# Attention in front of two feed-forward layers: the first chunk divided by its softmax sums after the products with values, sums and their spread from TensorE, a new order

## The chip, the cores and the metric

The kernel runs on one core of a Trainium2 chip. The metric is the device time of one execution in microseconds. The engines are TensorE (PE; its weight loads are shown apart as PEld), VectorE (DVE), ScalarE (ACT), GpSimd (POOL) and SyncE (SP), which here issues the transfers (DMA).

## The reference

All numbers are fp32. Attention has 2 batches, 8 heads, 768 tokens and 64 dimensions a head. Each token sees the tokens nearer than 16 positions, and besides these 24 block keys (maxima over 32 keys), to whose scores log 32 is added, with block values (means over 32 values). The result, 1536 tokens by 512, goes through a gated layer of 1536 hidden units and a second layer of 2048.

```python
k_sum = k.reshape(B, H, nb, block, D).max(axis=3)
v_sum = v.reshape(B, H, nb, block, D).mean(axis=3)
scores_l = where(|i - j| < 16, scale * q @ k.T, -1e9)
scores_s = scale * q @ k_sum.T + log(block)
a = exp(scores_all - max); a = a / (sum(a) + 1e-09)
x = a @ concat([v, v_sum])            # -> (1536, 512)
x = (silu(x @ w_gate) * (x @ w_val)) @ w_out
h = x @ w_in                          # second layer
g = where(h >= 1, h, where(h <= -1, 0, (h + 1)**2 / 4))
out = g @ w_out2
```

## The kernel before

The 1536 tokens are cut into three chunks of 512. Chunk 0 goes through both layers in a plain form; chunks 1 and 2 are done together later in a form that needs fewer products. Attention works on pairs of heads (four) and segments of 256 tokens (two per chunk), so chunk 0 has eight segment jobs. In each, four windows of 64 queries meet 120 keys: 96 neighbours and 24 blocks (KN = 120).

A segment job is a row of stages, each a function in `stages`: `sc`, the scores on TensorE, two PSUM banks; `mx`, on VectorE, masks and scales a tile of 128 rows (two heads' windows) at a time, and takes the extremes, into `sm`; `ex`, the exponentials on ScalarE; `su`, the row sums on VectorE, in the first four segment jobs only (`wide`), while the others let ScalarE accumulate the sums; `iv`, the reciprocals; `no`, the multiplication of the weights with the reciprocals, on VectorE or GpSimd; `wt`, four transposes on TensorE; `pt`, the copy of the transposed weights to SBUF (`pT`). Then `av` multiplies them with the window's values, and for chunk 0 `xh` and `xl` split the result, channels by tokens, into a high and a low part, each in the reduced-precision format fp32r in which TensorE multiplies the layers (three products for one: high with high, high with low, low with high, `mm3`). `ve` puts the means of the block values beside the neighbours' values; `av` needs it. Weights of the layers are decoded from 64-bit words (`high`, `low`, `bits`) and split (`hi`, `lo`).

The order of all instructions is made by a planner (`Plan.emit`) when the program is built. It takes, again and again, the ready job with the least of planned start plus `urge` times rank, and puts it on the engine with the least of start plus a weighted cost. The ranks, and the jobs' times, are the constants of table `T` and the numbers in braces at each job. Rings (score tiles, PSUM banks, slots of SBUF) hold a job back until its place is free; chunk 0 may use eight banks, since the accumulators of the layers are not open then. Where the planner foresees that TensorE will wait, `bank` (line 296) puts in up to 14 transposes of the identity, the padding. Engines serve their queues in the planned order; semaphores make them wait where the plan was wrong.

Lines that the following speaks of: 296 padding; 577 `av`; 594 `xl`; 626 `sc`; 639 `mx`; 645 `su`; 651 `ex`; 657 and 659, 660 `iv`; 664 `no`; 672 `wt`; 385, 387 and 389 the helper `copy` on ScalarE, GpSimd and VectorE; 918 the helper `subtract`; 979 the products with the layers' weights; 483 the means of values; 514 the transposes of keys; 558 those of queries.

Of the kernel before, what the change touches and what calls it, by code (L numbers as in the profile page):

```python
# [25 lines left out]
 'urge': 0.00031,  # L26
 'weight': (0.672, 366.647, 0.107, 0.393),
# [3 lines left out]
 'd': (1603.21, 21201.717),  # L31
 'load': (2535.858, 1169.195),
 'high': (-317.411, 144.375),
 'bits': (-9479.17, 323.65),
 'keep': (-8824.092, -1262.662),
 'read': -21513.508,
 'hi': (-1775.607, 438.05),
 'lo': (1720.695, -1280.083),
 'head_rank': (-928.987, -10909.065, -11298.818, 1371.39),
 'half_rank': -8764.036,  # L40
 'start': 146.833,
 'unit': 2.295,
 'e0': 140.493,
 'a1': (66.347, 15.995),
 'a2': (120.489, 10.661),
 'x': (326.313, 950.529),
 'j': (573.745, 3379.756),
 'g': (0.575, 58.663),
 'q': (0.02, 0.075),
 'jr': (223.915, 25.793),  # L50
 'jw': (526.692, 905.968),
 'rw': 1427.588,
 'js': (-12378.664, 1097.852),
 'gh': (305.541, 615.993),
 'gl': -803.961,
 't': 255.967,
 'th': 1363.181,
 'tl': -46.182,
 'qp': (-25.993, -0.438, 3.895, 62.512, 43.492, -4.889, -18.174),
 'qf': 37.334,  # L60
 'qj': -997.531,
 'qa': 1676.758,
 'rs': 755.395,
 'rh': 472.89,
 'x2': 62.301,
 'r2': (-105.0, 2012.755),
 'first': (641.149, 531.258),
 'st_q': (2394.976, -370.146),
 'st_qt': (595.066, -1246.954),
 'st_sc': (-351.835, -992.682),  # L70
 'st_mx': (-696.018, -1785.299),
 'st_ex': (-1399.05, 2957.286),
 'st_iv': (-4718.413, -828.92),
 'st_no': (616.963, -14960.718),
 'st_wt': (-628.517, 19.831),
 'st_pt': (-29498.836, 337.373),
 'st_av': (213.136, -938.929),
 'st_xh': (-1380.886, -2003.135),
 'st_xl': (-1030.954, -12578.763),
 'kl': (-42201.382, -2356.932),  # L80
 'kp': (2529.629, -2690.699),
 'kt': (-5799.683, 2883.66),
 'km': (-12751.053, -745.621),
 'kc': (1095.192, -13449.83),
 'vl': (3292.292, -1209.876),
 'vm': (2875.792, 2369.738),
 'vs': -8200.552,
 'vo': (-8471.926, -9352.02),
 've': (-19.098, 1391.293),
 'ql': (-21759.128, -1085.432),  # L90
 'wl': (-2925.377, -25041.841),
 'wide': 4,
 'st_su': (810.604, 7542.977),
 'seg': (129.041, -64.326),
 'ko': (-3502.726, 21290.576)}
# [136 lines left out]
def tile_block_attention_ffn(  # L232
# [20 lines left out]
    nc = tc.nc  # L253
# [23 lines left out]
    ap_ = ctx.enter_context(tc.tile_pool(name="ap", bufs=2))  # L277
# [9 lines left out]
        "qT": 2, **T["rings"],  # L287
# [58 lines left out]
    for m, offs in enumerate(((0, WINDOW), (WINDOW, WINDOW), (WINDOW, 2 * WINDOW))):  # L346
# [9 lines left out]
        "big1", (1, (2 * WPS, H, D)), (2, (CH,)), (2, (2, S // P, D)), (2, (2 * D,)), (1, (2, NB + 32)), (1, (NB + 32,)))  # L356
    vall, qTs, kraws, vms, wavg, tavg = carved[0], carved[1:3], carved[3:5], carved[5:7], *carved[7:]
# [8 lines left out]
    n_steps, n_jobs = [0], [0]  # L366
# [178 lines left out]
    xt = {}  # L545
# [20 lines left out]
    def values(c, p, tag, one=None):  # L566

        px = bank(tag, "px")
        pend["px", c, p] = pend["px", c, p, one] = px
        for i, (b, s) in enumerate(chunk_segments(c)):  # L570
            if one not in (None, i):
                continue
            pT, vwin = pend.pop(("pT", b, s, p)), vwins[(b * NSEG + s) % 2]
            for w in range(WPS):
                col = i * SEG + w * QT
                for h in range(2):
                    nc.tensor.matmul(  # L577
                        px[h * D:(h + 1) * D, col:col + QT], vwin[0:KN, w, 2 * p + h],
                        pT[0:KN, 2 * h + w // 2, w % 2 * QT:(w % 2 + 1) * QT],
                        start=True, stop=True,  # L580
                    )
# [7 lines left out]
    def values_lo(c, p, i, *rings):  # L589
        x = xt[c][p]  # L590
        if rings:
            x.append(slot(rings[0], f"xl{p}", F32R))
        cols = slice(i * SEG, (i + 1) * SEG)
# [10 lines left out]
    def stages(b, s, p, wide, first=None):  # L604

        c, col = divmod(b * S + s * SEG, CH)
        v_ = shared[b, s, p] = {}

        def scores(*tags):
# [4 lines left out]
            v_["mx"] = ap_.tile([P, 2, WPS], F32, tag="mx", name="mx", bufs=4)  # L614
# [53 lines left out]
        def weights(tag, ring):  # L668
            v_["pT"] = pend["pT", b, s, p] = slot(ring, "pT").rearrange("p (w c) -> p w c", c=P)
            pt = v_["pt"] = bank(tag, "pt")  # L670
            for w in range(WPS):
                nc.tensor.transpose(pt[0:KN, w * P:(w + 1) * P], v_["sm"][:, w], ident)  # L672

        def weights_out(engine):
            pT = v_["pT"]
            copy(engine, pT[0:KN].rearrange("p w c -> p (w c)"), v_["pt"][0:KN, :])
# [3 lines left out]
            "ex": exps, "su": sums, "iv": inverse, "no": normalise,  # L680
            "wt": weights, "pt": weights_out,
# [7 lines left out]
        ("su", {"DVE": 0.65}, "st_su", ("ex",)),  # L689
# [3 lines left out]
        ("pt", {"ACT": 0.61, "DVE": 0.69}, "st_pt", ("wt",)),  # L693
    )
# [43 lines left out]
    def step_jobs(c, p, t, banks, after):  # L738
# [22 lines left out]
        if not c:  # L761
            for i, (b, s) in enumerate(segs):
                u = t + T["seg"][0] * i
                h = (*n, i)
                job(("av", *(h if not i else n)), {"PE": 0.56},
# [3 lines left out]
                av, xh, xl = (("av", *n), ("xh", *n), ("xl", *n)) if i else (  # L769
                    ("av", *h), ("xh", *h), ("xl", *h))  # L770
                job(xh, {"ACT": 0.4, "DVE": 0.42}, u + T["st_xh"][0],
                    lambda e, *rings, i=i: values_hi(c, p, i, e, *rings),
                    [av] + ([("xh", *n, 0)] if i else []), () if i else (XS,))
                job(xl, {"DVE": 0.42}, u + T["st_xl"][0],
                    lambda e, *rings, i=i: values_lo(c, p, i, *rings),
                    [xh] + ([("xl", *n, 0)] if i else []), () if i else (XS,), [(av, 0)])
# [22 lines left out]
    def segment_jobs(b, s, p, t, banks, done):  # L799
# [15 lines left out]
        wide = n_jobs[0] < T["wide"]  # L815
        n_jobs[0] += 1
        fns = stages(b, s, p, wide, one)
        for name, engines, dt, needs in STAGES:
            fn = fns[name]
            if name == "su" and not wide:  # L820
                continue
            if wide and name == "ex":
                engines = {"ACT": 0.95}
            if wide and name == "iv":
                engines, needs = {"DVE": 0.18}, ("su",)
            rank = plan.jobs["sc", *one][1] + 0.1 if one and name == "sc" else t + T[dt][c > 0]
            job((name, *n), engines, rank,
                (lambda e, *tags, fn=fn: fn(*tags)) if "PE" in engines else lambda e, *_, fn=fn: fn(e),
# [653 lines left out]
```

## Time and profile before

| | us |
|---|---|
| median of 3 runs | 613.23 (612.58 to 614.61) |
| the profiled execution | 613.35 |
| its span in the profile | 611.6 |

| engine | busy us | share of the span |
|---|---|---|
| PE | 599.6 | 98% |
| PEld | 494.2 | 81% |
| DVE | 493.2 | 81% |
| ACT | 359.1 | 59% |
| POOL | 35.9 | 6% |

The profile is one execution. Times in it count from the start of its span. A busy engine is one that has an instruction in work; matmuls overlap, and their ends are modelled, so a busy TensorE need not be one at its peak. The granted clock is TensorE's, 1.00 being 2.4 GHz and 0.50 being 1.2 GHz.

### The profile page before, as it was taken

Reading aid. Unit: us, or ns where it says so; the run is one execution under the profiler, and the core shown is the slowest. Engines: PE = TensorE matmul, PEld = TensorE weight load, DVE = VectorE, ACT = ScalarE, POOL = GpSimd, SP = SyncE. Lnnn points to the kernel's source line nnn. Section 1 sums busy time; section 2 is a strip of 40 time slices with the busy share of each in tenths; the row PEclk is TensorE's granted clock in tenths of the full one; section 3 lists DMA queues with packets and bytes.
Section 4 is the critical chain, followed back from the end, with each engine's and each line's share of the span. In section 5 each row is a group of like instructions: output and inputs, shape, how many; then the busy total and the mean of one; then the engine's idle time right before and its main releaser. Section 6 shows DMA issues by size and latency. Waiting matters only on the chain.

```text
span 611.6 us, 9465 instructions
## 1 busy us (share of the span) xinstructions
PE 599.6 (98%) x3554; PEld 494.2 (81%) x3554; DVE 493.2 (81%) x897; ACT 359.1 (59%) x650; POOL 35.9 (6%) x55
## 2 busy tenths in 40 slices
PE   7889999999999999999999999999999999999997
PEld 6588888888878888888888888888888888888886
DVE  5789888999898998998888878788888868857662
ACT  5886678878888874764444444332278565556112
POOL 4250001100000000000000001000000010001000
PEclk9799999999999999999999999999999999999999
DMA  9999999998999670441120221133310420021411
GB/s 217 285 267 249 340 318 358 370 338 284 253 315 308 234 275 1 173 145 62 69 70 0 70 105 69 35 103 104 137 36 0 128 80 35 0 70 45 163 35 69
DMA packets 82334, 94.99 MB, mean 155 GB/s; under 512 B 40432, under 2 KB 65264, under 8 KB 82288
## 3 DMA queue, kind: packets, MB, share of 16 engines
q1 hardware_dynamic: 82288, 94.39, 48.1%
q8 instruction: 28, 0.46, 0.3%
q14 instruction: 18, 0.15, 0.1%
HBM read 73.40 MB, written 20.97 MB: 154 GB/s over the span
## 4 chain that ended last, share of the span: by engine, by line
PE 93%; DVE 3%; ACT 1%; DMA 1%; SPq 1%; issue 0%; POOL 0%; ACTq 0%; DVEq 0%; POOLq 0%
PE acc_y L979 38%; PE qi L979 12%; PE qv L979 9%; PE qg L979 9%; PE pi L979 7%; PE pv L979 5%; PE pg L979 5%; PE px L577 2%; PE pt L672 1%; PE sc L626 1%; DMA big<-in_k_dram 1%; DVE wb L895 1%; DVE wA L389 1%; SPq L439 1%; PE pk L296 1%; ACT sm L651 1%
## 5 line engine op out<-in xcount | busy, mean ns | idle before, releaser
L979 PE MATMUL acc_y<-dd,h 128*128 128x512 f32 (+1 forms) x387 | 88.9, 387 | 0.0
L979 PEld LDWEIGHTS acc_y<-dd,h 128*128 128x128 f32 x387 | 72.4, 188 | 14.9
L979 PE MATMUL acc_y<-h,dd 128*128 128x512 f32 x288 | 66.5, 389 | 0.0
L385 ACT ACTIVATE dd<-wf 128x1024 fp32r<-128x1024 f32 x25 | 26.4, 1058 | 62.8 <-PE acc_y L979 62.8
L979 PEld LDWEIGHTS acc_y<-h,dd 128*128 128x128 f32 x288 | 54.1, 188 | 11.3
L979 PE MATMUL acc_y<-wA,h 128*128 128x512 f32 x192 | 46.3, 391 | 0.0
L979 PE MATMUL qi<-xj,wjs 128*128 128x512 f32 x192 | 45.8, 389 | 0.0
L979 PE MATMUL pi<-y,wA 128*128 128x512 f32 x128 | 42.8, 394 | 0.0
L979 PEld LDWEIGHTS qi<-xj,wjs 128*128 128x128 f32 x192 | 36.0, 188 | 7.5
L979 PEld LDWEIGHTS acc_y<-wA,h 128*128 128x128 f32 x192 | 35.8, 188 | 7.4
L895 DVE SCALAR_TENSOR_TENSOR wb<-dd 128x1024 int32<-128x1024 int32 x34 | 41.1, 1220 | 0.3
L918 DVE TENSOR_TENSOR wA<-wb,wA 128x1024 fp32r<-128x1024 f32 x31 | 37.6, 1223 | 1.9 <-ACT wA L385 1.4
L886 ACT ACTIVATE dd<-raw 128x1024 f32<-128x1024 f32 x34 | 38.3, 1139 | 0.2 <-DMA raw<-in_moe_w_val_dram 0.2
L979 PE MATMUL acc_y<-h,wA 128*128 128x512 f32 x144 | 36.8, 399 | 0.0
L979 PE MATMUL qg<-xj,wjs 128*128 128x512 f32 x144 | 36.5, 389 | 0.0
L979 PE MATMUL qv<-xj,wjs 128*128 128x512 f32 x144 | 36.4, 389 | 0.0
L979 PE MATMUL pg<-x,wA 128*128 128x512 f32 (+1 forms) x112 | 35.4, 371 | 0.5 <-DVE wA L918 0.5
L979 PE MATMUL qi<-xj,wjo 128*128 128x512 f32 x144 | 34.7, 389 | 0.0
L979 PE MATMUL pv<-x,wA 128*128 128x512 f32 (+1 forms) x112 | 34.2, 368 | 0.0
L918 DVE TENSOR_TENSOR dd<-wf,dd 128x1024 fp32r<-128x1024 f32 x27 | 33.0, 1224 | 0.4 <-ACT dd L385 0.3
L918 DVE TENSOR_TENSOR h<-r,h 128x512 fp32r<-128x512 f32 x45 | 30.9, 691 | 1.2
L979 PEld LDWEIGHTS qi<-xj,wjo 128*128 128x128 f32 x144 | 27.0, 188 | 5.6
(167 smaller groups left out, 1216.3 us busy)
## 6 DMA issues: line engine op xcount, KB each, us to landing
raw<-in_moe_w_out_dram SPq DMA_DIRECT2D x14, 1024.0 KB, 7.3
raw<-in_moe_w_in_dram SPq DMA_DIRECT2D x16, 512.0 KB, 6.6
wf<-kept_z SPq DMA_DIRECT2D x16, 512.0 KB, 3.2
raw<-in_moe_w_gate_dram SPq DMA_DIRECT2D x12, 512.0 KB, 8.1
raw<-in_moe_w_val_dram SPq DMA_DIRECT2D x12, 512.0 KB, 8.6
kept_g<-wb SPq DMA_DIRECT2D x12, 512.0 KB, 5.5
wj<-kept_g SPq DMA_DIRECT2D x12, 512.0 KB, 4.5
wf<-kept_o SPq DMA_DIRECT2D x12, 512.0 KB, 3.4
```

Of the source, the lines that this page charges most:

```text
L296: nc.tensor.transpose(t[:, 0:P], ident, ident)
L385: nc.scalar.activation(out, in_, AF.Copy, scale=scale)
L389: nc.vector.tensor_copy(out, in_)
L439: nc.sync.dma_start(out=vwin[0:KW, w], in_=bass.AP(src.tensor, src.offset, [[D, KW], [S * D, H], [1, D]]),)
L577: nc.tensor.matmul(px[h * D:(h + 1) * D, col:col + QT], vwin[0:KN, w, 2 * p + h], pT[0:KN, 2 * h + w // 2, w % 2 * QT:(w % 2 + 1) * QT], s ...
L626: nc.tensor.matmul(scs[h][j * QT:(j + 1) * QT, w // 2], qT[head, (w + j) * QT:(w + j + 1) * QT], kwin[p][head, s * WPS + w + j], start=Tru ...
L651: nc.scalar.activation(sm[:, w], sm[:, w], AF.Exp, bias=mx[:, 0, w:w + 1], scale=-1.0, **more)
L672: nc.tensor.transpose(pt[0:KN, w * P:(w + 1) * P], v_["sm"][:, w], ident)
L886: nc.scalar.activation(x[:, 0], raws[k][:, :, :, 1].bitcast(F32), AF.Prelu, scale=2.0 ** -112, alpha=2.0 ** 32)
L895: nc.vector.scalar_tensor_tensor(b, x[:, 0], 3, x[:, 1], op0=ALU.logical_shift_left, op1=ALU.bitwise_or)
L918: e.tensor_tensor(out, a, b, op=ALU.subtract)
L979: nc.tensor.matmul(dst, lhs(a), rhs(b), start=first and i == 0, stop=last and i == 2, **more)
```

## The change

In chunk 0 the exponentials are transposed as they are, with one more row: column 121 of the score tile, which holds 1e-9. After the copy of the transposed weights TensorE multiplies each of the four tiles with a column of ones, which gives the sums over keys, rows by tokens, in the same PSUM bank (`dn`). VectorE takes their reciprocals (`iv`), and TensorE spreads these over the 64 channels of each head by products with the identity, into the upper half of that bank (`bc`), from where they are copied to SBUF (`rc`). The products with values run on weights that are not yet divided; `xd` multiplies their result with the spread reciprocals, and the split into high and low part starts from there. The stages `su` and `no` are gone for chunk 0, and its exponentials no longer accumulate. The low part may run on GpSimd, as may the high part. The bank of the transposed weights is given back behind `rc` instead of `pt`. The maxima and reciprocals get seven fixed places instead of a pool of four. The other chunks' segments keep the old stages. All constants of the order are new; of these the diff below shows the ones that rank the early transfers.

```diff
- 'urge': 0.00031,
- 'weight': (0.672, 366.647, 0.107, 0.393),
+ 'urge': 0.00016,
+ 'weight': (0.815, 163.313, 0.204, 0.389),
- 'load': (2535.858, 1169.195),
+ 'load': (3445.036, 776.002),
- 'first': (641.149, 531.258),
+ 'first': (-1897.243, 2032.421),
- 'kl': (-42201.382, -2356.932),
+ 'kl': (-36490.525, -5409.55),
- 'vl': (3292.292, -1209.876),
+ 'vl': (4534.176, -2102.256),
- 'ql': (-21759.128, -1085.432),
- 'wl': (-2925.377, -25041.841),
- 'wide': 4,
+ 'ql': (-31810.101, -2073.161),
+ 'wl': (-10648.491, -26648.057),
...
+    def values_scaled(c, p, i):
+        x, cols = scaled[c, p], slice(i * SEG, (i + 1) * SEG)
+        nc.vector.tensor_tensor(x[:, cols], pend.pop(("px", c, p, i))[:, cols], x[:, cols], op=ALU.mult)
...
-        copy(engine, xt[c][p][0][:, cols], pend["px", c, p, i][:, cols])
+        copy(engine, xt[c][p][0][:, cols], scaled[c, p][:, cols])
...
-        nc.vector.tensor_tensor(
-            x[1][:, cols], pend.pop(("px", c, p, i))[:, cols], x[0][:, cols].bitcast(F32),
-            op=ALU.subtract)
+        subtract(engine, x[1][:, cols], scaled[c, p][:, cols], x[0][:, cols].bitcast(F32))
...
-        def sums(engine):
-            nc.vector.tensor_reduce(v_["mx"][:, 1], v_["sum"], axis=AX.X, op=ALU.add)
+        def sums():
+
+            den = v_["den"] = v_["pt"][:, 0:WPS]
+            for w in range(WPS):
+                nc.tensor.matmul(
+                    den[:, w:w + 1], v_["pT"][0:KN + 1, w], ones, start=True, stop=True,
+                    skip_group_check=True)
+
+        def spread():
+
+            inv = v_["pt"][:, SEG:2 * SEG]
+            for x in range(WPS):
+                h, at = x // 2, x % 2 * P
+                nc.tensor.matmul(
+                    inv[h * D:(h + 1) * D, at:at + P], v_["mx"][:, 1, x:x + 1].to_broadcast([P, D]),
+                    ident, start=True, stop=True, skip_group_check=True)
+
+        def spread_out(engine, *rings):
+            i = col // SEG
+            if rings:
+                scaled[c, p] = slot(rings[0], "xs")
+            copy(engine, scaled[c, p][:, i * SEG:(i + 1) * SEG], v_["pt"][:, SEG:2 * SEG])
...
-                more = {} if wide else {"accum_out": v_["den"][:, w, 0:1]}
+                more = {"accum_out": v_["den"][:, w, 0:1]} if c else {}
...
-            if wide:
-                nc.vector.reciprocal(mx[:, 1], mx[:, 1])
+            if not c:
+                nc.vector.reciprocal(mx[:, 1], v_["den"])
                 return
...
-                nc.tensor.transpose(pt[0:KN, w * P:(w + 1) * P], v_["sm"][:, w], ident)
+                nc.tensor.transpose(
+                    pt[0:rows, w * P:(w + 1) * P], v_["sum"][:, w, 0:rows], ident)
...
+    EARLY = (
+        *STAGES[:2],
+        ("ex", {"ACT": 0.95}, "st_ex", ("mx",)),
+        ("wt", {"PE": 0.42}, "st_wt", ("ex",)),
+        STAGES[-1],
+        ("dn", {"PE": 0.45}, "st_dn", ("pt",)),
+        ("iv", {"DVE": 0.18}, "st_iv", ("dn",)),
+        ("bc", {"PE": 0.4}, "st_dn", ("iv",)),
+        ("rc", {"ACT": 0.4, "DVE": 0.42}, "st_rc", ("bc",)),
     )
...
+                job(xd, {"DVE": 0.42}, u + T["st_xd"],
+                    lambda *_, i=i: values_scaled(c, p, i),
+                    [av, ("rc", b, s, p)] + ([("xd", *n, 0)] if i else []), (), [(av, 0)])
-                job(xh, {"ACT": 0.4, "DVE": 0.42}, u + T["st_xh"][0],
+                job(xh, {"ACT": 0.4, "DVE+": 0.27, "POOL": 0.4}, u + T["st_xh"][0],
...
+        if not c:
+            gives["rc"] = gives.pop("pt")
+            takes["sc"] += (("mx",),)
+            gives["bc"] = [(("sc", *n), 3)]
...
+        for name, engines, dt, needs in STAGES if c else EARLY:
```

## Rows read from the trace of the kernel before

**Rows 1.** The page's part 1: each engine's busy us, share and instructions.
```profile
PE 599.6 (98%) x3554; PEld 494.2 (81%) x3554; DVE 493.2 (81%) x897; ACT 359.1 (59%) x650; POOL 35.9 (6%) x55
```

**Rows 2.** Stretches of the span: length, busy us per engine, granted clock, DMA share, GB/s.
```profile
4.70:18.20 13.50, 11.25 (x163) 8.66 (x162) 8.88 (x43) 9.56 (x30) 3.17 (x12) 1.00 1.23 228
18.20:30.50 12.30, 10.25 (x126) 7.32 (x126) 9.71 (x34) 9.29 (x30) 3.40 (x4) 0.72 1.01 301
30.50:38.80 8.30, 7.49 (x152) 6.55 (x152) 6.51 (x25) 7.10 (x21) 5.23 (x4) 1.00 1.03 277
38.80:49.80 11.00, 9.30 (x92) 8.04 (x91) 9.70 (x17) 8.80 (x19) 4.26 (x2) 1.00 0.88 279
49.80:262.00 212.20, 212.20 (x1486) 174.10 (x1485) 189.24 (x383) 164.51 (x320) 5.30 (x4) 1.00 0.82 269
```

**Rows 3.** The same stretches, padding of line 296 alone: PE, PEld, clock, DMA.
```profile
4.70:18.20 13.50, 1.98 (x11) 1.22 (x10) 1.00 1.23 228
18.20:30.50 12.30, 1.89 (x8) 1.22 (x8) 0.72 1.01 301
30.50:38.80 8.30, 1.09 (x8) 0.86 (x8) 1.00 1.03 277
38.80:49.80 11.00, 0.93 (x3) 0.42 (x3) 1.00 0.88 279
```

**Rows 4.** The stretch of the low clock, all engines.
```profile
19.30:26.10 6.80, 6.80 (x83) 5.09 (x81) 4.88 (x25) 4.74 (x20) 2.18 (x3) 0.51 1.01 300
```

**Rows 5.** Waits of TensorE, 30 to 90 us: total us, times, longest.
```profile
PE pq L558 <- DMA qraw<-in_q_dram: 1.2, 1, 1.2
PE pg L979 <- DVE wA L918: 0.5, 1, 0.5
PE pt L296 <- DVE xl L594: 0.5, 1, 0.5
PE pt L672 <- DVE sm L664: 0.3, 1, 0.3
```

**Rows 6.** TensorE in order of time: start, us, instruction, count.
```profile
43.25 0.60 PE L672 MATMUL pt<-ident,sm 128*120 128x128 f32 x4
43.61 0.36 PE L979 MATMUL pg<-x,wA 128*128 128x256 f32 x1
...
63.47 1.08 PE L483 MATMUL pv<-big 96*32 96x128 f32 x32
64.36 1.06 PE L483 MATMUL pv<-vrest,big 128*32 128x128 f32 x32
```

**Rows 7.** VectorE's groups, 0 to 50 us: count, busy us, mean ns.
```profile
L594 DVE TENSOR_TENSOR xl<-px,x 128x256 fp32r<-128x256 f32 x8 | 3.1, 413 | 0.7 <-ACT x L385 0.7
L664 DVE TENSOR_TENSOR big<-big,mx 128x480 f32<-128x480 f32 x3 | 2.0, 658 | 0.1
L664 DVE TENSOR_TENSOR sm<-sm,mx 128x480 f32<-128x480 f32 x1 | 1.7, 1734 | 0.0
L645 DVE TENSOR_REDUCE mx<-sm 128x4 f32<-128x484 f32 x2 | 1.3, 652 | 0.0
```

**Rows 8.** ScalarE in order of time: exponentials of two segments without accumulation.
```profile
10.19 2.39 ACT L651 ACTIVATE big<-big,mx 128x120 f32<-128x120 f32 x8
```

**Rows 9.** TensorE in order of time: transposed weights, padding, first product with weights.
```profile
14.24 0.65 PE L672 MATMUL pt<-ident,big 128*120 128x128 f32 x4
...
25.44 1.12 PE L296 MATMUL pt<-ident 128*128 128x128 f32 x5
26.41 0.60 PE L672 MATMUL pt<-ident,sm 128*120 128x128 f32 x4
...
38.83 0.39 PE L979 MATMUL pv<-x,wA 128*128 128x256 f32 x1
```

**Rows 10.** The chain that ended last, 0 to 70 us: start, us, what.
```profile
11.48 6.89 DMA big<-in_k_dram
...
23.27 3.03 ACT big L651 x16
```

More of the change, by code (lines that the diff above doesn't have):

```diff
@@ L85 @@
[L85 to L95 removed]
+ 'd': (-34091.663, 36248.122),
+ 'load': (3445.036, 776.002),
+ 'high': (-3309.64, 2281.678),
+ 'bits': (-9156.651, 266.286),
+ 'keep': (-20759.024, -12792.771),
+ 'read': -789.641,
+ 'hi': (-1495.869, 578.427),
@@ new lines @@
+ 'lo': (6193.222, -436.111),
+ 'head_rank': (-588.567, -22598.039, -24447.666, -13395.207),
+ 'half_rank': -24815.229,
+ 'start': 223.762,
+ 'unit': 2.062,
+ 'e0': 67.255,
+ 'a1': (66.375, 23.57),
+ 'a2': (172.697, 7.758),
+ 'x': (636.956, 97.652),
+ 'j': (612.844, 2094.702),
+ 'g': (0.763, 166.248),
+ 'q': (0.021, 0.07),
+ 'jr': (1265.451, 2056.738),
+ 'jw': (670.179, 1037.606),
+ 'rw': 2215.04,
+ 'js': (-18710.734, 3726.544),
+ 'gh': (147.231, 479.531),
+ 'gl': -720.733,
+ 't': 595.28,
+ 'th': 2041.25,
@@ L543, in kmax_out @@
         )
-    xt = {}
+    xt, scaled = {}, {}
     JOINT = (1, 2)
@@ L602, in values_out, with stages @@
         copy(engine, x, pend.pop(("px", c, p)))
-    def stages(b, s, p, wide, first=None):
+    def stages(b, s, p, first=None):
         c, col = divmod(b * S + s * SEG, CH)
+        n, rows = (b, s, p), KN + (not c)
         v_ = shared[b, s, p] = {}
@@ L671, in weights @@
             for w in range(WPS):
-                nc.tensor.transpose(pt[0:KN, w * P:(w + 1) * P], v_["sm"][:, w], ident)
+                nc.tensor.transpose(
+                    pt[0:rows, w * P:(w + 1) * P], v_["sum"][:, w, 0:rows], ident)
         def weights_out(engine):
             pT = v_["pT"]
-            copy(engine, pT[0:KN].rearrange("p w c -> p (w c)"), v_["pt"][0:KN, :])
+            copy(engine, pT[0:rows].rearrange("p w c -> p (w c)"), v_["pt"][0:rows, :])
         return {
             "sc": scores, "mx": maxima,
-            "ex": exps, "su": sums, "iv": inverse, "no": normalise,
-            "wt": weights, "pt": weights_out,
+            "ex": exps, "iv": inverse, "no": normalise,
+            "wt": weights, "pt": weights_out, "dn": sums,
+            "bc": spread, "rc": spread_out,
         }
@@ L814, in segment_jobs @@
             more["mx"] = [("sc", *two)]
[L815 to L818, printed above, removed]
-            fn = fns[name]
[L820 to L826, printed above, removed]
+        if not c:
+            gives["rc"] = gives.pop("pt")
+            takes["sc"] += (("mx",),)
+            gives["bc"] = [(("sc", *n), 3)]
+            if n == (0, 0, p):
+                takes["rc"] = (XF,)
+            else:
+                more["rc"] = [("rc", 0, 0, p)]
+        fns = stages(b, s, p, one)
+        for name, engines, dt, needs in STAGES if c else EARLY:
+            fn = fns[name]
+            rank = plan.jobs["sc", *one][1] + 0.1 if one and name == "sc" else t + (T[dt][c > 0] if isinstance(T[dt], tuple) else T[dt])
             job((name, *n), engines, rank,
-                (lambda e, *tags, fn=fn: fn(*tags)) if "PE" in engines else lambda e, *_, fn=fn: fn(e),
+                (lambda e, *tags, fn=fn: fn(*tags)) if "PE" in engines else lambda e, *rings, fn=fn: fn(e, *rings),
                 [(x, *n) for x in needs] + more.get(name, []),
```

122 lines of the change are left out of this document (53 added, 69 removed).

## The prediction

> **What bounds the kernel now.** I read the engines' shares first, then the stretches, then the waits of TensorE, then the start instruction by instruction. TensorE is busy 98% of the span [rows 1], and from 49.8 us to 262 us it is busy in every microsecond [rows 2]; no wait of TensorE lies behind 49.8. So each microsecond of TensorE work that the change adds behind that point is a microsecond of span, and all that an edit elsewhere can win lies ahead of it, where TensorE is idle, runs padding (transposes of the identity, line 296, which the planner puts into waits it foresees) or runs at half clock.
>
> That slack, by stretch (length minus TensorE's busy time [rows 2], then padding [rows 3]): 4.7 to 18.2 us: 2.25 idle, 1.98 padding; 18.2 to 30.5: 2.05 and 1.89; 30.5 to 38.8: 0.81 and 1.09; 38.8 to 49.8: 1.70 and 0.93. In 19.3 to 26.1 the granted clock is 0.51, the lower level of 1.2 GHz [rows 4]; five paddings lie there, about 1.0 us [rows 9], so the other 5.8 us of work would take some 2.9 at 2.4 GHz: another 2.9 us. Ahead of 30.5 this is 4.3 + 3.9 + 2.9 = 11.1 us of room, behind it 2.5 + 2.0 = 4.5 us. What lies ahead of 4.7 is setup and the first keys; nothing in the change touches it.
>
> The reader should see that the two rooms differ. Ahead of 30.5 TensorE waits for data: the DMA share is at 1.0 or over [rows 2], and the keys of the fourth pair, issued at 11.48, take 6.89 us to land [rows 10]. Attention's products with values and the first products with weights can't start there. Three of the eight chunk-0 segments have their weights transposed by then (three groups of four, the first at 14.24, the last at 26.41), and the first product with feed-forward weights comes at 38.83 [rows 9]. Behind 30.5 TensorE always has something to do or would have, if VectorE, ScalarE and GpSimd prepared it sooner: VectorE is busy 9.70 of 11.00 us from 38.8 to 49.8 [rows 2].
>
> **The change part by part.** *Removed, all in the eight segments of chunk 0:* four row sums over 484 elements on VectorE, 652 ns each, 2.6 us [rows 7]; eight normalisations, three of 658 ns and one of 1734 ns on VectorE, 3.7 us, the other four on GpSimd [rows 7]; the short sums over accumulators go as well, which I leave out of the sum. On ScalarE the exponentials of four segments lose the read of the accumulator: two segments take 2.39 us without it [rows 8] and 3.03 us with it [rows 10], so 0.32 us each, 1.3 us. *Added outside TensorE:* eight scalings of the product of 256 columns; the nearest row is the subtraction that reads the same bank, 413 ns [rows 7], so 3.3 us on VectorE. The low part is then read from SBUF instead of PSUM, at about the same price, and may go to GpSimd, as may the high part. The spread inverses must be copied out of PSUM, a copy of the same 256 columns, priced like the same row at 0.41 us, 3.3 us on ScalarE or VectorE. VectorE balance: 2.6 + 3.7 - 3.3 = 3.0 us less, if the copies go to ScalarE, which with 1.3 gone and 3.3 come pays 2.0 us more; about nothing on VectorE if they don't.
>
> *Added on TensorE, per segment:* four fp32 products with one column each (the sums), and four that spread the inverses over 64 rows by the identity. The trace has no such product. Other fp32 products that aren't transposes run as two instructions each, so eight and eight. Nearest from above: the transposes of 128 columns, which load weights of the same width as the sums do; four take 43.61 - 43.25 = 0.36 us, 0.09 us each [rows 6], so 0.72 us for eight. Nearest from below: the averages of values with 32 columns of weights; 32 take 64.36 - 63.47 = 0.89 us, 0.028 each [rows 6], 0.22 us for eight. For the sums I take 0.45, about the middle: their weights are as wide as in the upper row, their moving operand is shorter than in either. The spread loads 64 columns into two halves of the array, nearer to the lower row; I take 0.30 (bounds 0.22 and 0.72). Together 0.75 us a segment, 6.0 us for eight, bounds 3.5 and 11.5. The transposes carry one more row; that costs nothing that these rows show.
>
> The row shows transposes with a wide weight load at 90 ns each, whatever they move [rows 6]. The Trainium skill, page "TensorEngine Tiling (Array Packing)", section Instruction Overhead, says that a product with one moving column has the same latency as one with 60, and page "TensorE: Matmul & The Clock Gate", section LDWEIGHTS, prices a weight load at its columns over 1.2 GHz. By the second, an estimate, eight loads of 128 columns are 0.85 us and eight of 64 columns 0.43 us, 1.28 us a segment; the transposes' 90 ns with 120 columns lie a little under that rule's 100 ns. The sum with it is the fourth rival below.
>
> *Moved:* the transpose of a segment no longer waits for the sum, the inverse and the normalisation. That takes 0.65 + 0.66 us, the reciprocal and two hand-overs off the path from the exponentials to the transpose, and frees the ring of score tiles (four) sooner. The inverse moves behind TensorE's sums: copy of the transpose, sums, reciprocal, spread, copy, scaling. For an early segment this lies beside the wait for the averages of values; for the last one it is on the path, about 2 us longer. The sums and the spread are two new waits in TensorE's queue, which is served in order: behind them stand the next segments' scores and, after 38.8, the products with weights. The reciprocal is a new wait in VectorE's queue, ahead of other segments' maxima. The bank of the transposes is held until the copy of the spread, some 2 us more, out of eight banks.
>
> *The new order.* No DMA is added or dropped. Ranks count as rank times urge. In the old order this is keys -13.1, queries -6.7, windows of values -0.9, first weights 0.99, rest of values 1.02, second weights 1.31 (each from the table of constants at the top of the diff); in the new one -5.8, -5.1, -1.7, 0.25, 0.73, 0.90. The succession is the same, so I cost the DMA queue at nothing; GpSimd only loses work. If a window of values came ahead of the fourth pair's keys, that would cost what the keys wait.
>
> *The sum.* I expect six of eight segments to have transposes, sums and spread done by 30.5, three more than the three transposes of now, and the eighth segment's scores (0.5 us) as well. That brings 6 x 0.75 + 3 x 0.36 + 0.5 = 6.1 us into a room of 11.1, free of charge. Behind 30.5: two segments' new products, +1.5; work moved ahead, -1.6. Of the slack there I count as VectorE's: the waits for the low part (0.5), for a normalised tile (0.3) and for split weights (0.5) [rows 5], the 1.09 us of padding up to 38.8 and 0.4 of that behind it, 2.8 together; with VectorE 3.0 us lighter I take all of it back, -2.8. The wait for queries (1.2 [rows 5]) is a transfer's and stays. The longer path of the last segments and the new waits in TensorE's queue give some 0.7 back, an estimate of a third of the 2 us. Sum: 1.5 - 1.6 - 2.8 + 0.7 = -2.2. The profiled execution took 613.35 us (span 611.6 and 1.75 around it), so 611.15; it lies 0.1 above the median of 613.23, hence **611.1 us**.
>
> **The rivals.** *First, slower: the new products land where TensorE is short.* Place: 30.5 to 49.8. Price: 0.75 us for each segment whose sums and spread come there. If ScalarE, with 2 us more to do and busy 7.10 of 8.30 us from 30.5 [rows 2], delivers the transposed tiles no sooner than now, five segments are late, 3.75 us, none of the work moves ahead, and the new waits eat half of the 2.8 to be won: 3.75 - 1.4 = +2.35, **615.6**. At 1.84 us or more it counts as slower, so from (1.84 + 1.4) / 0.75 = 4.3 late segments on. For it: only three transposes lie ahead of 30.5 today, and the keys land late. Against it: the normalisation that held them is gone. Upper price: five times 1.44 would be 7.2 - 1.4 = +5.8.
>
> *Second, hidden anyway.* What ends the waits ahead of 38.8 is the landing of keys, values and weights; VectorE's lighter load isn't seen, and the new products just fill the room that there is: **613.2**. For it: DMA at 1.0 through this stretch [rows 2].
>
> *Third, the half clock goes too.* With six microseconds of products more between 12 and 27 us, TensorE doesn't run thin at 18 and the 2.9 us [rows 4] come back; all eight segments finish ahead of the products with values. Behind 30.5 then: no new products, 0.5 of scores and five transposes (1.8) moved, 2.8 recovered, 0.7 given back: -4.4, **608.8**; with the 1.2 us wait for queries gone as well 607.7.
>
> *Fourth, the weight loads set the price* (1.28 us instead of 0.75, two segments late): +1.1 on the forecast, **612.2**. The skill's rule speaks for it, the 90 ns row half.
>
> **How the numbers follow.** A measurement of this kernel tells about 0.3% (1.84 us) from no change. Forecast 0.42 (of it 0.32 faster, 0.10 within), first rival 0.22 (0.20 slower, 0.02 within), second 0.20 (within), third 0.11 (faster), fourth 0.05 (within). Faster 0.43, within 0.37, slower 0.20. The forecast's own range is 609.5 to 612.5; the range for 8 in 10 goes down to the third rival's far end, 607.7, and up past the first rival's 615.6 to 616.0, leaving out its dearest cases.
>
> **What would show it.** Right: six groups of transposes ahead of 30.5, padding behind 30.5 near nothing, the first product with weights ahead of 38.8, no normalisation or row sum on VectorE in chunk 0. The price: the start-to-start time of sixteen instructions, 0.75 us together. Wrong: TensorE waiting for the transposed copy, for the reciprocal or for a bank; idle time behind 50 us; the sums and the spread between products of 512 columns. The prediction fails if most of the sums come behind 30.5, or if their price is over 1 us.

## The result, and the profile after

The changed kernel takes 620.55 us (median of 6 runs, 618.31 to 622.80), against 613.25 for the kernel before beside it: ratio 1.0105, interval 1.0078 to 1.0132 over the runs that are compared. A second set, taken later with other runs, gave 620.84 us and 1.0139 (1.0105 to 1.0174). It is slower by some 7 us, where 2.1 us of gain were forecast. One run of an experiment below (the price put in late) had a mean granted clock of 0.56, took 1022.77 us and is left out of its ratio. The profiled execution took 620.16 us, its span is 618.5 us, 6.9 more than before.

The page's part 1 and the clock line of part 2 (the span in 40 slices, tenths of full speed), after the change:

```profile
PE 612.8 (99%) x3664; PEld 508.4 (82%) x3664; DVE 491.8 (80%) x890; ACT 353.0 (57%) x635; POOL 44.0 (7%) x62
PEclk9789999999999999999999999999999999999999
```

TensorE has 13.2 us more of busy time and 110 instructions more [rows 1]; VectorE and ScalarE have less to do, as the change meant. The stretches (length, busy us of PE, PEld, DVE, ACT, POOL, granted clock, DMA share, GB/s), after the change:

```profile
4.70:18.20 13.50, 13.50 (x159) 11.79 (x157) 7.34 (x39) 6.70 (x20) 3.50 (x12) 1.00 1.27 235
18.20:30.50 12.30, 12.07 (x121) 10.46 (x115) 4.24 (x13) 8.90 (x25) 0.00 (x0) 0.76 1.10 309
30.50:38.80 8.30, 8.30 (x156) 6.76 (x155) 4.52 (x32) 6.80 (x14) 4.32 (x7) 0.75 1.00 274
38.80:48.30 9.50, 9.50 (x148) 9.14 (x147) 7.43 (x22) 7.45 (x21) 3.37 (x4) 1.00 0.71 245
48.30:55.40 7.10, 6.84 (x52) 6.20 (x52) 6.45 (x8) 4.75 (x8) 3.23 (x3) 1.00 1.24 209
55.40:262.00 206.60, 206.60 (x1471) 168.96 (x1472) 182.28 (x379) 159.73 (x314) 10.51 (x5) 1.00 0.84 272
```

Against [rows 2]: TensorE's idle time between 4.7 and some 50 us fell from 6.8 us to 0.5, and VectorE, which was the busy one, does 4.24 us in 18.2 to 30.5 instead of 9.71. Ahead of 18.2 us it is not the change's products that fill TensorE's time: the first sum starts at 18.55. TensorE's old work is slower there. In this execution the second pair's key transposes take 1.76 us where the kernel before takes 1.0, so the clock was low up to some 12 us, although its row shows 1.00 (the last section has the lines). In another profile of the same order (the kernel with 64 columns, run again, see below), the second key transposes take the short time, TensorE is idle for 2.0 us in this stretch, and the third pair's key transposes start at 12.71 us instead of 15.10:

```profile
4.70:18.20 13.50, 11.47 (x167) 9.54 (x165) 6.06 (x31) 8.20 (x25) 3.13 (x12) 1.00 1.22 233
```

```profile
7.49 1.15 PE L518 MATMUL pk<-ident,kord 80*128 80x80 f32 x12
...
12.71 1.12 PE L518 MATMUL pk<-ident,kord 80*128 80x80 f32 x12
```

The first product with feed-forward weights comes at 48.28 us instead of 38.83 [rows 9], though by then all of chunk 0's attention is done. Behind 55.4 us nothing has changed: TensorE is busy all the time. Of TensorE's waits over the whole span (total us, times, longest) there are three left:

```profile
PE pk L297 <- POOL ident L307: 1.6, 1, 1.6
PE pt L654 <- ACT pT L389: 0.2, 1, 0.2
PE pg L1019 <- DVE wA L958: 0.2, 1, 0.2
```

What the new instructions cost stands in TensorE's order of time (start, us, instruction, count). L654 are the sums, L663 the spreads, L698 the transposes, after the change:

```profile
16.18 0.70 PE L698 MATMUL pt<-ident,big 128*121 128x128 f32 x4
...
18.55 1.05 PE L654 MATMUL pt<-big,pT 121*128 121x1 f32 x8 [0.23 <-ACT pT L389]
19.47 1.13 PE L518 MATMUL pk<-ident,kord 80*128 80x80 f32 x12
20.53 0.72 PE L698 MATMUL pt<-ident,big 128*121 128x128 f32 x4
21.06 1.03 PE L698 MATMUL pt<-ident,sm 128*121 128x128 f32 x4
...
26.56 0.68 PE L698 MATMUL pt<-ident,sm 128*121 128x128 f32 x4
27.17 1.41 PE L663 MATMUL pt<-ident,big 128*64 128x128 f32 x16
28.50 1.87 PE L654 MATMUL pt<-big,pT 121*128 121x1 f32 x8
30.23 1.09 PE L562 MATMUL pq<-ident,qraw 128*128 128x128 f32 x4
...
42.39 1.92 PE L654 MATMUL pt<-big,pT 121*128 121x1 f32 x16
44.24 1.15 PE L581 MATMUL px<-pT,big 120*64 120x64 f32 x32
45.32 1.05 PE L654 MATMUL pt<-big,pT 121*128 121x1 f32 x8
46.30 1.58 PE L663 MATMUL pt<-ident,big 128*64 128x128 f32 x24
47.66 0.69 PE L581 MATMUL px<-pT,big 120*64 120x64 f32 x16
```

Sixteen sum instructions take 44.24 - 42.39 = 1.85 us, 0.116 each, 0.93 us a segment; at half the clock eight take 30.23 - 28.50 = 1.73 us. Twenty-four spread instructions take 1.36 us, 0.057 each, 0.45 us a segment. Together 1.38 us, not 0.75. Added up from start to next start, the 64 sums take 8.3 us and the 64 spreads 4.8 us, 13.1 us with what the half clock puts on them. In the same way of counting, idle time shrank by 6.3 us, the padding (25 transposes instead of 43) by 2.1, and the rest of the attention's instructions grew by 1.5: 13.1 - 6.3 - 2.1 + 1.5 = 6.2 of the 6.9 us. Some 2 of the 6.3 us lie ahead of the first sum and went to the low clock of the start, not to new products.

### The profile page after: what moved, and what is told of

Its sections match the earlier page's. It is cut to its first block, busy times and chain, and to the rows that moved or that the text cites. A ratio compares the mean times of both kernels' runs of the same rounds, so it can differ in the third digit from the quotient of the medians.

```text
span 618.5 us, 9699 instructions
## 1 busy us (share of the span) xinstructions
PE 612.8 (99%) x3664; PEld 508.4 (82%) x3664; DVE 491.8 (80%) x890; ACT 353.0 (57%) x635; POOL 44.0 (7%) x62
## 4 chain that ended last, share of the span: by engine, by line
PE 97%; DVE 2%; ACT 1%; POOL 0%; issue 0%; ACTq 0%; POOLq 0%
PE acc_y L1019 37%; PE qi L1019 12%; PE qg L1019 9%; PE qv L1019 9%; PE pi L1019 7%; PE pg L1019 5%; PE pv L1019 5%; PE px L581 2%; PE sc L632 2%; PE pt L698 2%; PE pt L654 1%; PE pq L562 1%; PE pv L487 1%; PE pk L518 1%; PE pt L663 1%; PE pk L297 1%
## 5 line engine op out<-in xcount | busy, mean ns | idle before, releaser
L1019 PE MATMUL acc_y<-dd,h 128*128 128x512 f32 (+1 forms) x387 | 87.4, 387 | 0.0
L935 DVE SCALAR_TENSOR_TENSOR wb<-dd 128x1024 int32<-128x1024 int32 x34 | 43.3, 1286 | 1.6 <-ACT dd L926 0.9
L1019 PEld LDWEIGHTS acc_y<-wA,h 128*128 128x128 f32 x192 | 35.5, 188 | 7.3
L926 ACT ACTIVATE dd<-raw 128x1024 f32<-128x1024 f32 x34 | 38.8, 1148 | 0.0
L1019 PE MATMUL acc_y<-h,wA 128*128 128x512 f32 x144 | 35.0, 392 | 0.0
L389 ACT ACTIVATE dd<-raw 128x1024 int32<-128x1024 uint32 x28 | 32.0, 1145 | 0.0
```

The lines of the kernel that those rows point to most:

```text
L389: nc.scalar.activation(out, in_, AF.Copy, scale=scale)
L926: nc.scalar.activation(x[:, 0], raws[k][:, :, :, 1].bitcast(F32), AF.Prelu, scale=2.0 ** -112, alpha=2.0 ** 32)
L935: nc.vector.scalar_tensor_tensor(b, x[:, 0], 3, x[:, 1], op0=ALU.logical_shift_left, op1=ALU.bitwise_or)
L1019: nc.tensor.matmul(dst, lhs(a), rhs(b), start=first and i == 0, stop=last and i == 2, **more)
```

## The experiments

The theories: *price*, that TensorE's new instructions cost more than the idle time could hold; *order*, that the new constants cost the time, since they delay the first products with weights; and, from the clock line, *half clock*. Times are medians with the ratio to the kernel before on the same chips.

**One sum of four, same order.** All other instructions stay where they were.

```diff
-            for w in range(WPS):
+            for w in range(1):
                 nc.tensor.matmul(
                     den[:, w:w + 1], v_["pT"][0:KN + 1, w], ones, ...)
-                nc.vector.reciprocal(mx[:, 1], v_["den"])
+                nc.vector.reciprocal(mx[:, 1], v_["den"][:, 0:1].to_broadcast([P, WPS]))
```

> The changed kernel in the very same order, but only the first of the four sums of a segment is made; its column serves for all four (48 of 64 instructions of TensorE left out, so three quarters of the divisors are another tile's). Theory A, price: each of these instructions takes 0.116 us at the full clock and more at half of it, 8.3 us for 64, so 48 give back 5.6 to 6.2: 614.4 to 615.0 us. Theory B, or the price of the forecast (0.056 an instruction): 2.7 at most, 617.9 us or more.

614.20 us, ratio 1.0018 (0.9991 to 1.0044): 48 instructions of this one kind are worth 6.3 us. That is the price theory's number, half clock included, and more than twice what the forecast's price allows. The order alone, which is the same here, can't be what costs the 7 us.

**One sum and two spreads, same order.**

```diff
-            for x in range(WPS):
+            for x in range(0, WPS, 2):
                 h, at = x // 2, x % 2 * P
                 nc.tensor.matmul(inv[h * D:(h + 1) * D, at:at + P], ...)
...
-            copy(engine, scaled[c, p][...], v_["pt"][:, SEG:2 * SEG])
+            copy(engine, scaled[c, p][...].rearrange("p (u t) -> p u t", u=2),
+                 v_["pt"][:, SEG:SEG + P].unsqueeze(1).to_broadcast([P, 2, P]))
```

> The kernel with one sum of four, and now also two of the four spread products of a segment left out (their columns are copies of the others, so the divisors are wrong). If the start is still bound by TensorE's own work, these 32 instructions of 0.057 us give back another 1.8 to 2.4 us: about 612 us. If it is bound by data (DMA, VectorE, ScalarE) once the sums are gone, the time stays at 614 us and TensorE is idle for longer.

613.38 us, ratio 0.9997 (0.9977 to 1.0017): another 0.8 us at most, not 2. With the sums mostly gone, further work taken from TensorE hardly pays. Some of TensorE's waits (total us, times, longest) in this kernel:

```profile
PE sc L632 <- issue: 0.4, 1, 0.4
PE pg L1020 <- DVE xl L959: 0.4, 1, 0.4
PE px L581 <- ACT big L389: 0.2, 1, 0.2
PE pg L1020 <- DVE wA L959: 0.2, 1, 0.2
```

So the waits for VectorE that the forecast meant to win are there again, in smaller pieces. A kernel of this form whose new products take 0.46 us a segment (two instructions of 0.116 and four of 0.057), less than the 0.75 of the forecast, is only level with the kernel before.

**64 columns of ones instead of one.** The same sums, at the same places, each 64 times over.

```diff
-            den = v_["den"] = v_["pt"][:, 0:WPS]
+            den = v_["den"] = v_["pt"][:, 0:SEG].rearrange("p (w c) -> p w c", c=D)
             for w in range(WPS):
                 nc.tensor.matmul(
-                    den[:, w:w + 1], v_["pT"][0:KN + 1, w], ones, ...)
+                    den[:, w], v_["pT"][0:KN + 1, w], ones.to_broadcast([KN + 1, D]), ...)
```

> The changed kernel in the very same order, but each sum is multiplied with 64 columns of ones in the place of one (the reciprocals read the first), so that each of the 64 products moves 64 columns. If the load of the 128 columns of weights sets the price of 0.116 us, nothing changes at the full clock: 619 to 622 us, as the changed kernel. If the one column set it (a product too short to pipeline), the price moves towards the 0.034 of the products with values: 616 or less. If the thin products are what the half clock follows, the stretches at 0.50 (22 to 24 us, 28 to 34 us) shorten, for up to 2.5 us less.

616.18 us, ratio 1.0064 (1.0040 to 1.0088): more multiplying, and 4 us less, where 2.5 at most were expected of the clock. The price of an instruction hasn't moved, as eight of them show in this kernel's order of time:

```profile
26.54 1.10 PE L654 MATMUL pt<-big,pT 121*128 121x64 f32 x8
27.48 0.60 PE L562 MATMUL pq<-ident,qraw 128*128 128x128 f32 x4
```

0.94 us for eight, 0.118 each, where one column took 0.116: up to 64 columns, what moves doesn't set it, which leaves the load of the weights. The clock has moved. Two stretches of this kernel, to be held against those after the change above (0.76 and 0.75):

```profile
18.20:30.50 12.30, 12.10 (x189) 10.51 (x191) 6.05 (x26) 10.95 (x29) 1.24 (x2) 1.00 1.01 300
30.50:38.80 8.30, 8.24 (x142) 7.30 (x137) 6.82 (x30) 8.24 (x22) 5.40 (x6) 1.00 1.05 294
```

**Both again, on one chip.** The changed kernel and the one with 64 columns, unaltered.

> The changed kernel once more, beside the next one on the same chip. If its half clock belongs to it and not to that day's chip: the recorded mean clock is 0.986 to 0.994 in nearly all runs and the time 618 to 623 us, longer by some 0.8 us for each us of span lost to the half clock.

> The changed kernel with 64 columns of ones once more. If the moving columns keep the clock up: most runs at a recorded 1.0 and 615.9 to 616.5 us, ratio to the kernel before about 1.005, 4 us below the changed kernel beside it. If the difference was a matter of chips: the same clock and time as the changed kernel.

620.84 us, ratio 1.0139 (1.0105 to 1.0174), and 616.99 us, 1.0058 (1.0036 to 1.0079). The recorded mean clock of the span in the twelve runs of the changed kernel is 0.977 to 0.994; in the fourteen with 64 columns it is 1.0 seven times, and 0.989 to 0.996 otherwise (in the second set 1.0 only twice in six, where most were expected). Over the changed kernel's runs the time goes from 618.31 us at 0.994 to 626.52 at 0.977: 8.2 us for 0.017 of 618 us, which is 10.5 us of clock lost, so 0.78 us for each. Carried on to 1.0 that is 615.4 us; the runs with 64 columns at 1.0 take 615.95 to 616.3. The kernel before at 1.0 takes 612.6 and 612.9. So at a recorded 1.0 the change costs 3 us, and the other 4 to 5 go with the half clock. A recorded 1.0 is not the full clock all the time: the profiled run with 64 columns has it, and its second pair's key transposes take 9.54 - 7.76 = 1.78 us, the slow time of the start.

**Sums from ScalarE, same order.** No sums on TensorE; the exponentials accumulate, as in the other chunks.

```diff
-                nc.tensor.matmul(den[:, w:w + 1], v_["pT"][0:KN + 1, w], ones, ...)
-                more = {"accum_out": v_["den"][:, w, 0:1]} if c else {}
+                more = {"accum_out": v_["den"][:, w, 0:1]}
...
-            if not c:
-                nc.vector.reciprocal(mx[:, 1], v_["den"])
-                return
```

> The changed kernel in the same order without the sums on TensorE: ScalarE accumulates them beside the exponentials (0.32 us a segment more, by the rows of before), VectorE adds them up and inverts them ahead of the spread. Theory, price of the sums: the 8.3 us of TensorE leave, room that can't be used stays as idle time, 2.6 us more on ScalarE: 611.5 to 614 us. If the loss were in the order or in the longer path behind the products: 618 or more.

616.61 us, ratio 1.0052 (1.0037 to 1.0067), 2.6 us over the upper end: a miss. Two of its stretches and three of TensorE's waits:

```profile
18.20:30.50 12.30, 10.84 (x149) 8.86 (x149) 6.32 (x24) 9.86 (x33) 0.47 (x1) 0.72 1.00 295
30.50:38.80 8.30, 7.85 (x127) 5.68 (x125) 6.86 (x39) 8.25 (x31) 6.19 (x7) 1.00 1.00 290
```

```profile
PE pk L518 <- DVE kord L393: 2.0, 1, 2.0
PE px L581 <- ACT pT L389: 0.7, 1, 0.7
PE pt L659 <- DVE big L678: 0.4, 1, 0.4
```

Four microseconds are gone from the changed kernel, a little over half of the loss. What keeps the rest isn't shown: TensorE waits 2.0 us for keys and 0.7 for a copy of ScalarE's, the half clock is back, and ScalarE is full (8.25 of 8.30 us), as it also is with 64 columns (8.24). In the ten runs the time goes with the clock again, from 617.77 us at 0.990 to 614.41 at 0.997.

**The price put into the kernel before.** Sixteen instructions of the new shapes, on constants, in each segment of chunk 0, with the old order; their results are written over. Once they stand ahead of the products with values, once ahead of the transposes.

```diff
+    def extra(out):
+        for w in range(WPS):
+            nc.tensor.matmul(
+                out[:, w:w + 1], ident, half_b, start=True, stop=True, skip_group_check=True)
+        for x in range(WPS):
+            h, at = x // 2, x % 2 * P
+            nc.tensor.matmul(
+                out[h * D:(h + 1) * D, at:at + P], half_b.to_broadcast([P, D]),
+                ident, start=True, stop=True, skip_group_check=True)
...
             pT, vwin = pend.pop(("pT", b, s, p)), vwins[(b * NSEG + s) % 2]
+            if not c:
+                extra(px[:, (1 - i) * SEG:(2 - i) * SEG])
```

> The kernel before in its own order, with sixteen instructions of TensorE more in each of the eight segments of chunk 0, of the shapes of the new sums and spreads (eight loads of 128 columns that move one, eight of 64 columns that move 128), on constants, ahead of the products with values; their results are written over. 0.116 and 0.057 us each at the full clock make 11.1 us. All stand behind 30.5 us, where the kernel before has 4.5 us of idle time and padding, of which padding stays: if TensorE's own time decides there, 613.2 + 11.1 less 0 to 2.5, 621.8 to 624.3 us. If the forecast's price (0.75 us a segment) were right: 616.7 to 619.2.

Ratio 1.0163 (1.0114 to 1.0212), three runs of 622.9 to 628.0 us: 10 us of the 11.1 are paid, 7 to 13 by the interval.

```diff
             pt = v_["pt"] = bank(tag, "pt")
+            if not c:
+                extra(pt[:, 0:SEG])
```

> The same sixteen instructions, now ahead of the transposes of each segment, so that three of eight segments have them ahead of 30.5 us. If the room ahead of 30.5 us takes what is put there free of charge, five segments pay: 613.2 + 5 x 1.39 = 620.2, less up to 2.5 us of idle time: 617.7 to 620.2 us, and at least 2 us less than with the products late. If the room can't be used, the time is that of the late ones.

619.48 us, ratio 1.0080 (1.0054 to 1.0107) against 614.42 of the kernel before on that chip: 4.9 us of the 11.1 are paid, half of what the late ones cost, as expected of a room that takes products free of charge. But the clock differs as well. The recorded mean is 0.986 to 0.989 in the late runs and 0.997 to 1.0 in the early ones; 0.011 of 620 us is 6.7 us of clock, and at the 0.78 us of the changed kernel for each that is 5 us, the whole difference. In the profiles the late products have a half clock more, in 30.5 to 38.8 us, and the early ones have none at all, not even the one of [rows 4]. The late ones first:

```profile
30.50:38.80 8.30, 8.30 (x93) 7.97 (x93) 2.40 (x12) 1.99 (x7) 4.58 (x3) 0.63 1.04 287
```

```profile
4.70:18.20 13.50, 13.50 (x129) 11.70 (x129) 8.29 (x35) 7.43 (x22) 3.19 (x12) 1.00 1.26 230
...
18.20:30.50 12.30, 11.27 (x193) 9.02 (x192) 8.71 (x40) 10.02 (x34) 2.40 (x3) 1.00 1.01 300
```

So what the early products won back is the half clock of 19 to 26 us, which the forecast had counted into that room; that idle time took the products isn't shown. The 13.50 busy us of 13.50, where it was 11.25 [rows 2], don't show it either: one segment's products lie there, 1.57 us, and the second key transposes take 9.76 - 7.99 = 1.77 us, the low clock of the start again:

```profile
7.99 1.84 PE L514 MATMUL pk<-ident,kord 80*128 80x80 f32 x12
9.76 1.88 PE L636 MATMUL sc<-big,big 64*64 64x120 f32 x32
```

**The division taken out of the kernel before.** No row sums, reciprocals and normalisation in chunk 0, old order.

```diff
         def sums(engine):
+            if not c:
+                return
...
         def inverse(engine):
             mx = v_["mx"]
+            if not c:
+                return
...
         def normalise(engine):
+            if not c:
+                return
```

> The kernel before in its own order without the row sums, the reciprocals and the normalisation of chunk 0 (its weights stay undivided there): VectorE loses 7 us and GpSimd 4 us of work up to 42 us, TensorE and the order stay. The forecast's step, that a lighter VectorE gives back the 2.8 us of waits and padding behind 30.5 us: padding is fixed in the order, so the three waits of 1.3 us at least, 610.5 to 611.9 us. If transfers and the fixed order set these waits, 612.7 to 613.5 us.

611.82 us, ratio 0.9960 (0.9941 to 0.9980): 2.5 us less than the kernel before beside it, 1.2 to 3.6 by the interval. A lighter VectorE is worth something, if nothing is put in its place; part of it may be the clock, recorded at 0.996 in the median against 0.993. The waits for split weights and for the low part are still there (total us, times, longest):

```profile
PE pg L985 <- DVE wA L924: 0.5, 1, 0.5
PE pt L296 <- DVE xl L594: 0.3, 1, 0.3
PE pg L985 <- DVE wA L389: 0.3, 1, 0.3
```

**The orders exchanged.** The old form with the new constants, and the new form with the old ones (the three new ranks scaled to the old urge).

```diff
 # old form
-T = {... 'urge': 0.00031, ...}
+T = {... 'urge': 0.00016, ..., 'wide': 4}
...
 # new form
-T = {... 'urge': 0.00016, ...}
+T = {... 'urge': 0.00031, ..., 'st_dn': -636.09, 'st_xd': -4820.82, 'st_rc': 10.59}
```

> The kernel before (division ahead of the transposes, no sums or spread on TensorE) with the new table of order constants. Theory A, price: the changed kernel is slower because its sums and spreads take 8.3 + 4.8 = 13.1 us of TensorE up to 48.3 us, where only 8.4 us of idle time and padding could be won. Then the order alone does little: 611 to 616 us. Theory B, order: the new order puts the first product with feed-forward weights at 48.3 us instead of 38.8, and this is what costs: 619 to 621 us here too.

> The changed kernel (sums and spreads on TensorE) with the old table of constants; the three new ranks are scaled to the old urge. Theory A, price: the 13.1 us on TensorE stay, 617 to 622 us. Theory B, order: the loss goes, 611 to 615 us.

634.89 us, ratio 1.0355 (1.0312 to 1.0398), and 638.68 us, 1.0403 (1.0372 to 1.0434). Neither theory has these numbers: both mixtures are 14 us and more above either kernel. The longest wait of TensorE behind the first few us, in the one and in the other:

```profile
PE pg L982 <- DVE wA L921: 7.0, 1, 7.0
```

```profile
PE pg L1020 <- DVE big L646: 4.8, 1, 4.8
```

A table of ranks belongs to the jobs that it was made for; with other jobs the planner puts a product ahead of data that come 5 to 7 us later, and TensorE's queue stands. So the exchange doesn't part order from form, and says nothing on whether the new order is good.

**Ones as weights.** The sums spread at once: the ones are the stationary operand, the transposed weights move, and VectorE inverts 256 columns.

```diff
-                    inv[h * D:(h + 1) * D, at:at + P], v_["mx"][:, 1, x:x + 1].to_broadcast([P, D]),
-                    ident, start=True, stop=True, skip_group_check=True)
+                    inv[h * D:(h + 1) * D, at:at + P], ones.to_broadcast([KN + 1, D]),
+                    v_["pT"][0:KN + 1, x], start=True, stop=True, skip_group_check=True)
...
-            copy(engine, scaled[c, p][:, i * SEG:(i + 1) * SEG], v_["pt"][:, SEG:2 * SEG])
+            nc.vector.reciprocal(scaled[c, p][:, i * SEG:(i + 1) * SEG], v_["pt"][:, SEG:2 * SEG])
```

> The changed kernel's order constants, but the sums come out spread at once: a block of ones of 64 columns is the stationary operand and the transposed weights (128 columns) move, eight instructions a segment in the place of sixteen; VectorE takes reciprocals of the 256 columns on the way to SBUF, and the reciprocals of four columns and the copy are gone. Theory A, price: the 8.3 us of sums leave TensorE, the 4.8 stay: about 612.3 us, less if the shorter path counts. Theory B, order: over 617 us. Rival: the reciprocal of 256 columns is dear on VectorE and its wait takes the place: 614 to 618.

634.08 us, ratio 1.0342 (1.0306 to 1.0379), far past the rival and within the order theory's open range, with an order that is a new one once more. The reciprocals (durations in ns, lowest, median, highest) and who waited for them:

```profile
L671 DVE RECIPROCAL xs<-pt x8: 1695/1748/1758, 20.6 to 46.0; 128x256 f32<-128x256 f32 x8
...
  PEld pg L297: 3.6, 1
  PE pg L297: 3.5, 1
```

1.75 us each, 14 us on VectorE, where a subtraction of the same columns takes 0.41 [rows 7]. Since two stages are gone, the planner also made another order from constants that weren't made for it, so the 14 us above the changed kernel can't be put down to the reciprocals alone.

## Why the prediction was wrong

**What bounds the kernel: right as to TensorE, open as to the two rooms.** Forty-eight sums less give 6.3 us, half clock included, and the late products cost 10 of their 11.1 (some 3 of these by the lower recorded clock, 0.988 in the mean against 0.9935 beside them). Behind 55.4 us nothing moved. That products ahead of 30.5 us are free and those behind it dear isn't shown: the early ones cost 4.9 us and the late ones 10, but by the slope of the changed kernel's runs the recorded clock alone accounts for that difference.

**The step that failed: the price of the sums.** I set 0.45 us a segment between two rows, and the upper one, the transposes' 0.72, was no upper bound: eight sums take 0.93. The spread took 0.45, not 0.30, inside its bounds. Together 1.38 instead of 0.75, five of eleven microseconds too few, and 0.06 short of my worst case; the price over 1 us that I had named as a sign of failure has come. The fourth rival was near the price. Its estimate from the Trainium skill, page "TensorE: Matmul & The Clock Gate", section LDWEIGHTS, eight loads of 128 columns and eight of 64 at 107 and 53 ns, was 1.28 us; the trace agrees within 8%, with 116 and 57 ns. I had counted that these products run as two instructions each, but let the short moving operand talk me below the weight load, though the 64-column run shows that the moving side plays no part up to there. The time of that rival was still wrong (612.2), because it had only two segments late.

**How many segments come early: wrong.** Six should have had transposes, sums and spread done by 30.5 us. The rows of after have four groups of transposes and four of sums there, and spreads for three; the profile with 64 columns, which has no half clock there, has the same, so it is the order and not the clock. The first rival named the place and the direction of the loss, with 615.6 us; with 1.38 us a segment in place of 0.75 its five late segments give 6.9 - 1.4 = +5.5, 618.8.

**The 2.8 us from a lighter VectorE: not borne out.** Taking the division out altogether, 7 us of VectorE with nothing in its place, gives 2.5, where the forecast took 2.8 from 3.0 us; by the pages VectorE has only 1.4 us less to do after the change. The change puts back a scaling and a copy out of PSUM for each segment; with three of four sums left out, so with a price of 0.69 us a segment (two instructions of 0.116 and eight of 0.057), below the forecast's, it still took 614.2 us instead of 611.1. These 3 us are this step and the count of early segments, which no run parts.

**The half clock: the other way.** The forecast's sum has no term for it: it counted the 2.9 us of [rows 4] as room and left them as they were, and the third rival let them go, as TensorE would be busier. TensorE is busier, and the half clock has grown: 20.9 to 25 us and 28 to 35.5 us at 0.58 and 0.55, some 5 us lost, where the kernel before lost 3.3 [rows 4]. The twelve runs' slope and the 64 columns, which keep the price and have no half clock on record in half of their runs, put 4 to 5 of the 7 us there and about 3 on the price less the room. In the kernel before the time goes with the clock too: its runs recorded at 0.997 take 612.1 to 614.84 us, those at 0.991 take 615.16 to 616.78. Of the 9.4 us between forecast and measurement, 4 to 5 go with the half clock; the other 5 are the price, the late segments and VectorE's share, which the runs part only by the 3 us that stay with the low price. Why the half clock grew stays open: the sums of one column go with it in the changed kernel, but the early products put into the kernel before have the same shapes at a recorded 0.997 to 1.0.

**The queue of transfers: right as costed.** Keys, queries, windows, first weights, the rest of values and second weights are issued in the same succession, and in the profiled execution, with its slow start, no wait of TensorE for a transfer is left. **The new waits in TensorE's queue** hardly showed there (for the transposed copy, 0.2 us). In the other profile of the same order, with the faster start, TensorE waits 1.1 us for that copy, 0.8 for keys and 0.2 for queries, so the 0.7 us set aside are not refuted.

## What to carry to other kernels

An operand of one column made a product no cheaper here than one of 64 columns, 0.116 against 0.118 us, and fp32 paid this twice: before work moves to TensorE, look at the columns of the stationary operand, count the instructions, and ask whether the operands can be exchanged. The count gives no exact price: the products with values, 64 columns of weights each, take 0.034 us (32 in 45.32 - 44.24 us above) where the spreads take 0.057. Put the new instructions, on constants, into the old kernel first, at the place they will have, and see what they cost. Compare the granted clock of the runs before explaining a difference by instructions or by their place: here it went with 4 to 5 of 7 us in the change, and, by the same slope, with the 5 us between early and late products. And check the clock row against the duration of a known instruction.

## What the runs showed of the hardware

The clock fell without a gap in TensorE's work: by the trace its last wait ahead of both falls, 0.23 us, ended at 18.55 us. After the sums of one column and the transposes of 18.5 to 21 us, the changed kernel's granted clock went to 0.58 in 20.9 to 25 us with TensorE busy 4.10 of 4.10; with 64 moving columns in the same places, the recorded clock of the whole span stayed at 1.0 in seven of fourteen runs. The kernel before with the early products, among them 64 of one column, was recorded at 0.997 to 1.0 in all four runs, so these rows don't tell what the clock goes by. The two low stretches of the changed kernel:

```profile
20.90:25.00 4.10, 4.10 (x50) 3.22 (x49) 0.59 (x3) 3.60 (x11) 0.00 (x0) 0.58 1.13 322
...
28.00:35.50 7.50, 7.50 (x97) 6.05 (x94) 3.38 (x16) 5.51 (x11) 2.09 (x2) 0.55 0.96 270
```

The clock row shows 1.00 ahead of the first change that is recorded, which need not be what was granted. In the changed kernel the second pair's key transposes take 9.69 - 7.93 = 1.76 us for twelve, in the kernel before the same twelve take about 1.0, and both rows show 1.00 there. So a recorded clock of 1.0 can hold a start at half speed:

```profile
7.93 1.83 PE L518 MATMUL pk<-ident,kord 80*128 80x80 f32 x12
9.69 1.11 PE L562 MATMUL pq<-ident,qraw 128*128 128x128 f32 x4
```

```profile
7.70 1.09 PE L514 MATMUL pk<-ident,kord 80*128 80x80 f32 x12
```

A reciprocal on VectorE takes 0.18 us for 4 columns and 1.75 for 256 columns of 128 rows, over four times the price of a subtraction of that size.
